# Attention and an eight-expert layer on one core: two output places used in turn, x and the routing logits in one row of 8 x 72, new step times

## The chip, the cores and the metric

One NeuronCore of a Trainium2 chip runs the whole program. The metric is device microseconds of one execution. The kernel before took 530.74 us, the median of three runs.

## The reference

The reference is an attention layer with a compressive memory, followed by a top-1 mixture of experts. There are B = 4 batches, H = 8 heads, S = 576 positions and D = 64 features of a head; then N = 2304 tokens of 512 features, E = 8 experts and F = 1024 hidden features.

```python
def _attn_ref(q, k, v, M_prev, z_prev, beta):
    scores = scale * np.matmul(q, k.transpose(0, 1, 3, 2))
    scores = np.where(causal, -1000000000.0, scores)
    scores = scores - scores.max(-1, keepdims=True)
    a = np.exp(scores)
    a /= a.sum(-1, keepdims=True) + 1e-09
    local = np.matmul(a, v)
    q_p = phi(q)
    mem_out = (q_p @ M_prev) / (q_p @ z_prev + 1e-06)
    g = 1.0 / (1.0 + np.exp(-beta))
    return g * mem_out + (1 - g) * local

def _moe_ref(x, w_gate, w1, w2):
    logits = x @ w_gate
    expert_idx = np.argmax(logits, axis=1)
    gate_w = softmax(logits)[expert_idx]
    for e in range(E):
        xe = x[expert_idx == e]
        out[expert_idx == e] = gate_w * (np.maximum(xe @ w1[e], 0.0) @ w2[e])
```

## The kernel before, in words

The program has two stages that follow each other. Attention runs from the start to about 276 us, the experts from there to the end.

**Attention** (`attention`) works on 8 groups g, each one batch and four heads, and 16 units u of two heads. For a group, q, k and v are loaded (`load`, L248 and L249, issued by SyncE), cast to 16 bits in two parts (`cast_k` L256 and L257, `cast_q` L265), and transposed by DMA (`trans`, L288, with a copy of half of it in L291) or, for the first ones, on TensorE (`ptm`, L302, L346, copied out in L305, L309, L348). `phi` (L276 to L281) makes the features for the memory. For a unit, `n_steps` makes row maxima (scores `sn` on TensorE, L375 and L381; maxima on VectorE, L383, L398, L407, L410, L411), which enter the queries as an extra column (`QT`, by DMA in L404 or on TensorE as `ptq`, L425 and L426); `s_steps` makes the scores `st` (L462), their exponentials on ScalarE (L481) and the causal cut on GpSimd (L466); `p_steps` multiplies with v (L536); `d_steps` adds up rows (`sm`, L567, evicted by ScalarE in L574). The features of v carry 8 more columns, so that a head's output has 64 numbers of x and 8 of the routing logits, 72 in all.

`m_steps(g)` has five steps, one for each tile of 128 positions (the fifth has 64). It makes the memory's part in PSUM (`ps`, 4 heads of 73), the norm (L607, L608), and two VectorE multiplies: L612 writes the 64 features of four heads into `xb` (or `xt` for the fifth tile), L614 the 8 logits of each head into `lgp`. `a_steps(g)` makes the denominators (`den`, L630 and L633, and `rl`, L635 to L639), then five times the local part (`loc`, L652), its scaling on VectorE (`lt`, L655, four heads of 72) and two additions: L659 on GpSimd to x, L662 to `lgp`, on GpSimd too but on VectorE for the last group. For each second group L668 and L670 add the logits up over the heads, and SyncE stores x to DRAM (`x_scratch`, L673 and L678). The routing (`r_...` tiles, L960 to L1076) makes ranks, tables (`r_tab`, L1051, evicted to `r_gate` in L1056 and L1057) and the token lists.

The order of all this is not that of the code. Every step has a time, computed from the table K and shifted by the entries of `sh`; the steps are sorted by it (L867), TensorE follows that list as it stands, and the other engines and the DMA queue of SyncE follow what a scheduler makes of it.

**The experts** (`experts`) are written by hand with semaphores. A turn takes 128 tokens of one expert: GpSimd gathers their rows of x (L1375), VectorE (L1586) and GpSimd (L1422) split them into two 16-bit parts, SyncE transposes them by DMA (L1298), TensorE multiplies with the first matrix (p1, L1474) and the second (p2, L1490; L1487 in a turn of 64 tokens). ScalarE evicts the result from PSUM to `ysb` (`m_y`) with the gate as its scale (L1536, or two halves in L1532), GpSimd copies the token numbers (L1399) and scatters the rows to the output (L1393). Between these, ScalarE (L1159) and VectorE (L1163) convert the next expert's weights, loaded in L1271.

There is one `ysb`. Before an eviction, ScalarE waits until the scatter before it has landed (`rr.w("sc", 16, 16)`); before a p2, TensorE waits until the eviction before it is done (`PE.wait_ge(S["ya"], yw)`). The last scatter takes its token numbers from a copy made ahead of the wait for the eviction (L1440). The first turn's x is transposed on TensorE (`m_px`, L1460).

Of the kernel before, what the change touches and what calls it, by code (L numbers as in the profile page):

```python
# [6 lines left out]
F32 = mybir.dt.float32  # L7
# [15 lines left out]
         k1=-0.85, setup=2.0, v1=2.35, sw=(3.0, 3.05, 3.1, 3.4), sm=(2.9, 3.5, 3.65), cast=-1.0, castd=0.0, tk=-0.35,
         tq=-0.45, phi=0.8, pt=1.95, lk=-1.9, lq=-1.8, lv=0.75, n=(-0.15, 0.75), s=(1.05, 2), p=(2, 3.05), m0=(4.2,
         4.1), m7=(3.35, 3.45), m=(2.6, 3.7), a0=(4.4, 4.85), a=(4, 5.2), wl=(14.4, 14.3, 15.2, 15.5, 17.0, 17.2,
         17.2, 17.6), wc=(15.8, 16.4, 16.5, 17.1, 17.3, 17.3, 18.2, 18.25), sh=dict(cast_q30=0.3, m_steps1w=0.25,
         wconv01=-0.37, load2k=-0.67, s_steps14w=-0.02, a_steps4=0.2, const_q1=-0.08, n_first68=-0.14, first_q2=0.02,
         m_steps2w=-0.15, p_steps2w=0.22, wload03=-0.05, wconv03=-0.72, s_first12=0.47, setup=-0.06, n_steps4=0.03,
         s_steps6w=-0.77, p_steps0=-0.09, s_steps13=0.03, n_steps8=-0.05, cast_k20=0.15, phi21=0.88, wload06=0.12,
         p_steps4w=0.55, a_steps1=0.15, s_steps8w=0.77, wload10=0.48, load6k=-0.18, p_steps7=0.02, s_steps4=-0.07,  # L30
         setup_w0=-0.03, n_steps15=-0.35, load4k=-0.02, n_steps13=0.17, n_steps2w=-0.2, load5q=0.25, wload02=0.03,
         p_steps12w=0.13, bothtrans_piece1=-0.03, trans3QT1=0.05, load6v=0.03, load2v=-0.28, load4q=0.08,
         wload13=-0.75, wload01=0.58, s_steps12=0.03, load1k=-0.8, m_steps7w=-0.9, s_steps1w=0.15, s_first01=0.05,
         load_pieceq0=-0.64, n_first56=0.08, p_steps1w=-0.35, m_steps5w=0.12, load0v=0.06, n_steps11=-0.43,
         load_piecek1=-0.45, wload05=-0.02, p_steps15w=0.08, n_steps12w=-0.4, s_steps3=-0.17, wconv00=-0.1,
         a_steps6w=-0.25, p_steps8w=-0.85, trans2QT1=-0.07, n_steps11w=0.05, load1q=0.6, cast_q50=0.03,
         p_steps12=0.05, p_steps9w=-0.1, phi51=0.2, wconv02=0.4, load5k=-0.12, wconv06=-0.32, phi40=-0.23,
         n_steps13w=-0.03, trans7KT1=-0.05, n_first89=0.01, phi60=-0.08, cast_q71=-0.12, setup_m2=0.05, cast_k01=0.1,
         phi50=-0.9, a_steps7=0.2, cast_q20=0.2, n_steps7=0.06, cast_q40=0.03, m_steps4=0.77, p_steps4=-0.1,
         p_steps13w=-0.4, trans7QT1=-0.02, s_first37=0.43, const_k2=-0.35, load3k=0.05, load_piecek0=-0.45,  # L40
         m_steps3=0.95, first_k2=-0.02, s_steps10w=-0.84, p_steps1=-0.06, wload04=0.1, load6q=0.05, cast_k10=0.2,
         load0k1=0.2, setup_m1=0.4, setup_w3=-0.2, p_steps13=0.4, s_steps8=0.03, setup_w2=-0.03, a_steps0w=-0.1,
         phi70=-0.7, setup_z1=0.2, wload12=0.15, a_steps3w=-0.03, s_steps9=-0.03, trans0PT=-0.01, trans4PT=-0.08,
         p_steps14=0.35, p_steps5=0.06, load4v=0.73, setup_z0=0.2, phi10=-0.08, trans2PT=-0.01, p_steps0w=-0.9,
         n_steps12=0.15, cast_k11=0.05, p_steps9=-0.1, const_k0=-0.02, load3v=-0.05, cast_q60=-0.4, wload17=0.77,
         n_steps15w=0.45, a_steps3=0.2, load3q=0.25, const_rest=-0.4, p_steps6w=-0.03, wconv05=-0.03, trans6KT1=0.13,
         phi61=-0.04, wconv04=0.17, wload07=-0.35, m_steps7=-0.43, phi01=0.15, trans4KT1=-0.07, a_steps2=-0.13,
         a_steps2w=0.43, m_steps5=0.1, s_steps12w=0.15, s_steps14=0.03, p_steps10=-0.2, n_steps4w=0.05, wload11=0.03,
         wload16=-0.03, cast_q41=0.05, cast_q21=0.03, trans5QT1=-0.2, a_steps7w=-0.1, load_piecek2=-0.77,
         s_steps7=-0.2, p_steps11w=0.07, cast_q51=-0.1, phi41=0.8, wload00=0.2, s_steps9w=0.05, p_steps8=0.7,  # L50
         bothcast_piece2=0.03, n_steps5w=-0.03, load_pieceq2=-0.8, a_steps5w=0.1, p_steps5w=0.33, s_steps1=-0.05,
         trans7PT=0.4, wconv10=0.86, m_steps4w=-0.05, cast_k50=0.05, p_steps6=0.05, s_steps13w=-0.03, load7v=-0.05,
         s_steps7w=-0.08, phi30=-0.05, s_steps4w=0.03, s_steps15=0.1, s_steps11=0.05, load5v=-0.03, m_steps6w=-0.77,
         trans3KT1=-0.05, n_first1011=0.2, p_steps10w=0.45, cast_k71=0.03, phi11=-0.2, n_steps1w=-0.03, trans6QT1=0.2,
         p_steps14w=-0.1, p_steps7w=0.83, cast_k41=-0.2, p_steps11=-0.2, d_steps3w=0.4, setup_z2=-0.4, trans3PT=-0.4,
# [1586 lines left out]
```

## Time and profile before

| | |
|---|---|
| three runs | 527.58, 530.74, 534.57 us |
| the profiled execution | 530.83 us |
| its span, first to last instruction | 529.1 us |
| mean granted TensorE clock | 0.975 |
| TensorE busy | 480.2 us, 91% of the span |
| VectorE, ScalarE, GpSimd busy | 344.1, 225.6, 260.9 us |
| instructions | 14122 |

Times in the rows are microseconds from the first instruction unless they say ns. PE is TensorE (PEld its weight load), DVE is VectorE, ACT is ScalarE, POOL is GpSimd, SPq is SyncE's issue of DMAs. A row of a timeline gives start, duration, engine, line, operation, output <- input and, in brackets, how long the engine stood idle before it and what ended that. "issue" is idle time in which the engine waited for nothing that the profile shows. The granted clock is given as a share of full speed, 2.4 GHz.

### The profile page before, as it was taken

Reading aid. Unit: us, or ns where it says so; the run is one execution under the profiler, and the core shown is the slowest. Engines: PE = TensorE matmul, PEld = TensorE weight load, DVE = VectorE, ACT = ScalarE, POOL = GpSimd, SP = SyncE. Lnnn points to the kernel's source line nnn. Section 1 sums busy time; section 2 is a strip of 40 time slices with the busy share of each in tenths; the row PEclk is TensorE's granted clock in tenths of the full one; section 3 lists DMA queues with packets and bytes.
Section 4 is the critical chain, followed back from the end, with each engine's and each line's share of the span. In section 5 each row is a group of like instructions: output and inputs, shape, how many; then the busy total and the mean of one; then the engine's idle time right before and its main releaser. Section 6 shows DMA issues by size and latency. Waiting matters only on the chain.

```text
span 529.1 us, 14122 instructions
## 1 busy us (share of the span) xinstructions
PE 480.2 (91%) x5235; PEld 323.7 (61%) x5235; DVE 344.1 (65%) x805; ACT 225.6 (43%) x360; POOL 260.9 (49%) x482
## 2 busy tenths in 40 slices
PE   4899899997989999999976999699999989999992
PEld 2454455754556565656645677477667767776872
DVE  3778686974758386889886786567752348772331
ACT  6577663753537364567523334245301033600110
POOL 5748756773729255737234343524433333453441
PEclk9989999998989999999997999999999999999997
DMA  5568969699896989996424879967896239432430
GB/s 131 126 129 170 152 146 180 145 222 159 127 190 170 169 166 176 210 290 230 164 89 86 249 249 303 238 204 230 279 269 172 93 64 299 128 109 59 100 75 26
DMA packets 169854, 89.56 MB, mean 169 GB/s; under 512 B 151855, under 2 KB 151855, under 8 KB 169776
## 3 DMA queue, kind: packets, MB, share of 16 engines
q1 hardware_dynamic: 165856, 77.62, 62.3%
q0 software_dynamic: 3920, 11.02, 6.9%
q8 instruction: 35, 0.57, 0.5%
q14 instruction: 43, 0.35, 0.2%
HBM read 54.56 MB, written 11.27 MB: 124 GB/s over the span
## 4 chain that ended last, share of the span: by engine, by line
PE 40%; issue 16%; DMA 13%; POOL 13%; DVE 7%; SPq 5%; ACT 3%; POOLq 1%; ACTq 0%; DVEq 0%
PE m_ph L1474 7%; PE o L536 6%; DMA out_dram<-m_y,m_is 5%; PE m_py L1490 5%; PE st L462 5%; PE sm L567 3%; DMA mem<-mem 3%; PE loc L652 3%; PE sn L375 2%; POOL m_xg L1375 2%; POOL m_xn L1422 2%; POOL out_dram L1393 2%; DMA QT<-mem 2%; POOL xb L659 1%; DMA m_xB<-m_xn 1%
## 5 line engine op out<-in xcount | busy, mean ns | idle before, releaser
L1474 PE MATMUL m_ph<-m_xT,mem 128*128 128x128 f16 (+1 forms) x1536 | 79.6, 214 | 7.6 <-issue 5.3
L1474 PEld LDWEIGHTS m_ph<-m_xT,mem 128*128 128x128 f16 x1536 | 77.7, 99 | 12.3 <-issue 7.1
L1579 DVE TENSOR_SCALAR m_hT<-m_ph 128x512 f16<-128x512 f32 (+1 forms) x46 | 29.1, 632 | 78.7 <-PE m_ph L1474 64.1
L1536 ACT ACTIVATE m_y<-m_py,m_gc 128x512 f32<-128x512 f32 x18 | 12.4, 688 | 132.0 <-PE m_py L1490 69.5
L1422 POOL TENSOR_TENSOR m_xn<-m_xg,m_xn 128x512 f16<-128x512 f32 x23 | 26.5, 1152 | 84.6 <-DVE m_xn L1586 84.6
L383 DVE TENSOR_REDUCE mt<-sn 128x2 f32<-128x512 f32 (+4 forms) x83 | 53.8, 666 | 21.6 <-PE sn L381 18.0
L481 ACT ACTIVATE aT<-st 128x512 f32<-128x512 f32 x96 | 55.5, 595 | 26.5 <-PE st L462 22.6
L1490 PE MATMUL m_py<-mem,m_hT 128*128 128x512 f16 x288 | 64.5, 379 | 1.3 <-issue 1.0
L466 POOL TENSOR_SCALAR_AFFINE_SELECT aT<-aT 128x128 f32<-128x128 f32 (+2 forms) x160 | 43.9, 292 | 39.8 <-ACT aT L481 38.0
L536 PE MATMUL o<-aT,mem 128*64 128x320 f32 (+4 forms) x320 | 59.3, 433 | 1.4 <-POOL aT L466 1.4
L462 PE MATMUL st<-mem 128*128 128x64 f16 (+5 forms) x224 | 46.9, 265 | 1.8 <-ACT aT L481 1.7
L1490 PEld LDWEIGHTS m_py<-mem,m_hT 128*128 128x128 f16 x288 | 27.5, 98 | 33.1 <-DVE m_hT L1579 1.3
L462 PEld LDWEIGHTS <-mem 128*128 128x128 f16 (+1 forms) x448 | 32.9, 101 | 17.0 <-issue 5.6
L462 PE MATMUL st<-QT,mem 66*128 66x64 f16 (+5 forms) x224 | 43.1, 265 | 0.1
L1474 PE MATMUL m_ph<-m_xT,m_w 128*128 128x128 f16 (+1 forms) x672 | 37.9, 220 | 4.7 <-issue 4.7
L1474 PEld LDWEIGHTS m_ph<-m_xT,m_w 128*128 128x128 f16 x672 | 37.1, 100 | 6.7 <-issue 5.5
L375 PE MATMUL sn<-mem 128*128 128x256 f16 (+3 forms) x158 | 32.5, 284 | 7.0 <-DMA mem<-mem 3.2
L1393 POOL DMA_INDIRECT out_dram<-m_y,m_is x24 | 27.7, 1153 | 21.8 <-POOL m_is L1399 12.8
L1375 POOL DMA_INDIRECT m_xg<-x_scratch,m_ig x24 | 28.5, 1187 | 19.0 <-POOL m_ig L1415 16.8
L536 PEld LDWEIGHTS o<-aT,mem 128*64 128x64 f32 x320 | 25.4, 137 | 17.4 <-issue 9.6
L659 POOL TENSOR_TENSOR xb<-lt,xb 128x256 f32<-128x256 f32 x32 | 25.3, 794 | 15.7 <-DVE lt L655 11.0
L1490 PE MATMUL m_py<-m_w,m_hT 128*128 128x512 f16 x144 | 32.2, 379 | 0.5 <-issue 0.4
(249 smaller groups left out, 943.6 us busy)
## 6 DMA issues: line engine op xcount, KB each, us to landing
mem<-in_moe_w_dram SPq DMA_DIRECT2D x40, 512.0 KB, 5.8
m_stage<-in_moe_w_dram SPq DMA_DIRECT2D x24, 512.0 KB, 6.4
mem<-in_q_dram SPq DMA_DIRECT2D x32, 128.0 KB
mem<-in_k_dram SPq DMA_DIRECT2D x32, 128.0 KB
mem<-in_v_dram SPq DMA_DIRECT2D x32, 128.0 KB
x_scratch<-xb SPq DMA_DIRECT2D x4, 1024.0 KB
mem<-mem SPq DMA_DIRECT2D x6, 288.0 KB
m_xB<-m_xn SPq DMA_TRANSPOSE x46
```

The source lines that it names most:

```text
L375: nc.tensor.matmul(ps[:, c:c + k1 - k0], QT[:, 5 * hh + t, :], keys(hh)[:, k0:k1], start=(c == 0), stop=(k1 == parts[-1][3] and hh == part ...
L383: nc.vector.reduce_max(out, v, axis=AX.X)
L462: nc.tensor.matmul(ps[:, c:c + n], kk[:, kb, :], qq[:, w:w + n], start=(first and i == 0 and j == 0), stop=(last and i == 1 and j == len(p ...
L466: nc.gpsimd.affine_select(out=ap, in_=ap, pattern=pattern, compare_op=ALU.is_ge, fill=0.0, base=base, channel_multiplier=-1)
L481: nc.scalar.activation(out=a, in_=ps, func=AF.Exp, scale=ESC)
L536: nc.tensor.matmul(o[64 * hh:64 * hh + 64, q0:q0 + n], vv, aa, start=(j == 0), stop=(j == 4), skip_group_check=True)
L659: nc.gpsimd.tensor_tensor(out=x, in0=tmp[r, :, 0:64], in1=x, op=ALU.add)
L1375: G.indirect_dma_start(out=x, out_offset=None, in_=x_dram, in_offset=bass.IndirectOffsetOnAxis(ap=i, axis=0), bounds_check=bound, oob_is_e ...
L1393: G.indirect_dma_start(out=out, out_offset=bass.IndirectOffsetOnAxis(ap=i, axis=0), in_=ysb, in_offset=None, bounds_check=bound, oob_is_er ...
L1422: G.tensor_tensor(out=xn[1], in0=xg, in1=xn[0], op=ALU.subtract).then_inc(S["xl"], 1)
L1474: mm = PE.matmul(ph[i2][:, f, 0:N], w[:, kc, c:c + 128], xT[:, x, kc, 0:N], start=(i == 0), stop=(i == 11), skip_group_check=True)
L1490: mm = PE.matmul(py, hh, ww[:, 4 + ff // 2, c:c + 512], start=st, stop=sp_)
```

## The change

First, `ysb` has two places, taken in turn, with a semaphore each (`sc0`, `sc1`). An eviction waits for the scatter two before it, in a branch that picks the place; GpSimd's `send` has the same branch and holds the copy of the token numbers, so that the copy ahead for the last scatter is gone. Second, x and its logits lie in rows of 8 heads of 72: `lgp` is gone, one VectorE multiply of 4 x 72 takes the place of L612 and L614, and one GpSimd add of 4 x 72 that of L659 and L662, for the last group too. The DRAM rows grow from 512 to 576 numbers, the gather brings all of them, and the splits read them 64 out of 72. The first turn's x goes through eight TensorE operations of a head each instead of four of 128 columns. Third, some 60 entries of the table K change.

```diff
@@ K
-         wc1=(...), nc3=2, cuts=((1, 2), (0, 1)), rc=7.75, r0=(16.1, 18.45),
-         k1=-0.85, setup=2.0, v1=2.35, ...
+         wc1=(...), nc3=2, cuts=((1, 2), (0, 1)), rc=7.75, r0=(16.0, 18.65),
+         k1=-1.2, setup=1.6, v1=2.4, ...
...
@@ m_steps
-                nc.vector.tensor_tensor(out=x[:, 64 * h0:64 * h0 + 256].rearrange("p (h d) -> p h d", d=64),
-                                        in0=ps[r, :, 0:64], in1=nrm[r].to_broadcast([n, 4, 64]), op=ALU.mult)
-                nc.vector.tensor_tensor(out=lgp[r, t, h0:h0 + 4, :], in0=ps[r, :, 64:72],
-                                        in1=nrm[r].to_broadcast([n, 4, 8]), op=ALU.mult)
+                nc.vector.tensor_tensor(out=x[:, h0:h0 + 4], in0=ps[r, :, 0:72], in1=nrm[r].to_broadcast([n, 4, 72]), op=ALU.mult)
@@ a_steps
-                x = x[:, 64 * h0:64 * h0 + 256].rearrange("p (h d) -> p h d", d=64)
-                nc.gpsimd.tensor_tensor(out=x, in0=tmp[r, :, 0:64], in1=x, op=ALU.add)
-                lp = T["lgp", b][r, t, h0:h0 + 4, :]
-                eng = nc.gpsimd if g < NG - 1 else nc.vector
-                eng.tensor_tensor(out=lp, in0=tmp[r, :, 64:72], in1=lp, op=ALU.add)
+                x = (xb[:, t] if t < 4 else xt[r])[:, h0:h0 + 4]
+                nc.gpsimd.tensor_tensor(out=x, in0=tmp[r], in1=x, op=ALU.add)
...
@@ experts
-    ysb = sb.tile([128, 512], F32, name="m_y")
+    ysb = sb.tile([128, 2, 512], F32, name="m_y")
...
-        def send(i):
+        def send():
+            def of(j):
+                i = isc[:, j:j + 1]
+                G.tensor_copy(out=i, in_=ids[:, col("c3")]).then_inc(S["iscp"], 1)
+                G.wait_ge(S["iscp"], reg["g"])
+                G.sem_inc(S["pw"], 1)
+                G.reg_add(reg[f"ns{j}"], reg[f"ns{j}"], 16)
+                G.indirect_dma_start(out=out, out_offset=bass.IndirectOffsetOnAxis(ap=i, axis=0), in_=ysb[:, j],
+                                     in_offset=None, bounds_check=bound, oob_is_err=False).then_inc(S[f"sc{j}"], 16)
             G.sem_inc(S["pw"], 1)
-            G.reg_add(reg["ns"], reg["ns"], 16)
...
+            with G.If(G.snap(reg["y"]) < 1):
+                of(0)
+                G.reg_mov(reg["y"], 1)
+            with G.Else():
+                of(1)
+                G.reg_mov(reg["y"], 0)
...
-        G.tensor_copy(out=ig0, in_=ids[:, col("c3")]).then_inc(S["iscp"], 1)
-        G.wait_ge(S["iscp"], reg["g"])
         G.wait_ge(S["ya"], reg["g"])
-        send(ig0)
-        G.wait_ge(S["sc"], reg["ns"])
+        send()
...
-        for c in range(4):
-            mm = PE.transpose(px[:, c], xg0[:, 128 * c:128 * c + 128], ident)
+        for h in range(8):
+            mm = PE.matmul(px[64 * (h % 2):64 * (h % 2) + 64, h // 2], xg0[:, h, 0:64], ident, start=True, stop=True, skip_group_check=True)
...
             rr.w("gcp", 1)
-            rr.w("sc", 16, 16)
+            def to(j):
+                A.wait_ge(S[f"sc{j}"], free)
...
+            with A.If(A.snap(odd) < 1):
+                to(0)
+                A.reg_mov(odd, 1)
+            with A.Else():
+                to(1)
+                A.reg_mov(odd, 0)
+                A.reg_add(free, free, 16)
```

What the table moves is seen in the engines' own orders. VectorE in the first 25 us, around the extra column of the first queries, before (`mt0` the maxima, `IW` a table of constants; L257 is the cast of k's second part):

```order
L407 TENSOR_TENSOR mt0_114<-mt0_114 128x5
L383 TENSOR_REDUCE mt0_114<-sn_262 128x1
L410 TENSOR_SCALAR mem81921_60<-mt0_114 128x5
L257 TENSOR_TENSOR mem81920_59<-mem81920_59 128x9x64
L411 SCALAR_TENSOR_TENSOR mem81921_60<-mt0_114,mem81921_60 128x5
L167 COPY IW_517<-ident_66 64x4x64
L309 COPY mem92162_61<-ptm_302 128x1024
```

And now, where the lines stand 3 higher:

```order
L410 TENSOR_TENSOR mt0_114<-mt0_114 128x5
L386 TENSOR_REDUCE mt0_114<-sn_262 128x1
L413 TENSOR_SCALAR mem81921_60<-mt0_114 128x5
L170 COPY IW_462<-ident_66 64x4x64
L414 SCALAR_TENSOR_TENSOR mem81921_60<-mt0_114,mem81921_60 128x5
L170 COPY IW_462<-ident_66 64x4x64
L260 TENSOR_TENSOR mem81920_59<-mem81920_59 128x9x64
L312 COPY mem92162_61<-ptm_281 128x1024
```

The cast of k's second part moved behind the instruction that completes the extra column (L411 before, L414 now); a small copy of constants stands in its place.

SyncE's queue in the middle of attention, around the store of the first batch's x, before (`mem` places are the casts, their transposes, and k, q or v as loaded):

```order
L249 DMA mem92162_61<-in_v_dram 128x1x64
L673 DMA x_scratch<-xb_930 128x4x512
L288 DMA_TRANSPOSE mem81921_60<-mem81920_59 128x18x128
L288 DMA_TRANSPOSE mem92162_61<-mem81920_59 128x18x128 x2
L248 DMA mem81920_59<-in_k_dram 128x4x64
L404 DMA_TRANSPOSE QT2_1815<-mem81921_60 128x9x128
L291 DMA mem81921_60<-mem92162_61 64x2304
L248 DMA mem81920_59<-in_k_dram 128x4x64
```

And now:

```order
L252 DMA mem92162_61<-in_v_dram 128x1x64
L407 DMA_TRANSPOSE QT2_1515<-mem81921_60 128x9x128
L291 DMA_TRANSPOSE mem81921_60<-mem81920_59 128x18x128
L667 DMA x_scratch<-xb_919 128x4x576
L291 DMA_TRANSPOSE mem92162_61<-mem81920_59 128x18x128 x2
L294 DMA mem81921_60<-mem92162_61 64x2304
L407 DMA_TRANSPOSE QT2_1825<-mem81921_60 128x9x128
L251 DMA mem81920_59<-in_k_dram 128x4x64 x2
```

One of the three transposes moved ahead of the store, and the k load that stood between the transposes and the transpose of the queries moved behind both.

TensorE at the end of attention, before (`sm` the row sums, `r_tab` the routing's table, `den` the denominators, `loc` the local part, `r_warm` matmuls whose results nobody reads):

```order
L567 MATMUL sm<-aT,ones 32x64 x4
L1051 MATMUL r_tab<-e,aT 128x288 x2
L1051 MATMUL r_tab<-q_3925,aT 128x288 x2
L1051 MATMUL r_tab<-e,aT 128x288
L630 MATMUL den<-ident,sT 128x128 x4
L633 MATMUL den_3951<-ident,sT 128x4
```

And now:

```order
L570 MATMUL sm<-aT,ones 32x64 x4
L1045 MATMUL r_tab<-q_3775,aT 128x288 x2
L629 MATMUL den<-ident,sT 128x128 x4
L632 MATMUL den_3851<-ident,sT 128x4
L1045 MATMUL r_tab<-e,aT 128x288
L651 MATMUL loc<-IW,oT 128x144 x4
L1045 MATMUL r_tab<-e,aT 128x288
L651 MATMUL loc<-IW,oT 128x144 x4
L1045 MATMUL r_tab<-q_3870,aT 128x288
```

Three of the five table rows that stood between the sums and the denominators now stand between and behind the local parts. On VectorE the two copies out of the table (L1056 and L1057, now L1050 and L1051) moved with them, from ahead of the denominators to between the logits' sums (L662, L664) and the first step of the ranks (L961, before L967).

## Rows read from the trace of the kernel before

**Rows 1.** Windows: start:end, length; busy time (instructions) of each engine; clock, DMA share, GB/s
```profile
25.00:250.00 225.00, 212.06 (x2067) 128.68 (x2066) 167.44 (x477) 131.83 (x229) 134.42 (x303) 0.98 0.85 177
290.00:529.00 239.00, 219.50 (x2784) 164.40 (x2784) 132.28 (x187) 63.23 (x76) 94.84 (x134) 0.98 0.62 175
342.00:350.00 8.00, 8.00 (x102) 7.38 (x100) 3.48 (x5) 4.58 (x5) 1.41 (x3) 0.79 1.04 228
```

**Rows 2.** Waits: engine, line, what for, total us, times, longest us
```profile
PE m_ph L1474 <- issue: 10.0, 6, 4.4
...
ACT mem L1159 <- issue: 3.6, 4, 1.4
```

**Rows 3.** Timeline of the first 25 us, SyncE, ScalarE, TensorE and VectorE
```profile
5.52 0.54 SPq L249 DMA_DIRECT2D mem<-in_q_dram  x1
...
9.27 1.16 ACT L265 ACTIVATE mem<-mem 128x1152 f16<-128x1152 f32 x1 [0.38 <-DMA mem<-in_q_dram]
...
12.26 0.26 PE L375 MATMUL sn<-mem 128*128 128x128 f16 x1 [2.33 <-ACT mem L348]
...
20.57 1.86 DVE L257 TENSOR_TENSOR mem<-mem 128x576 f16<-128x576 f32 x1
...
22.67 0.44 PE L425 MATMUL ptq<-mem 128*128 128x128 f16 x5 [1.00 <-DVE mem L411]
```

**Rows 4.** Timeline around 121 us, TensorE
```profile
121.11 0.38 PE L375 MATMUL sn<-mem 128*128 128x128 f16 x4 [1.13 <-DMA mem<-mem]
125.46 0.19 PE L501 MATMUL st<-QT,mem 66*128 66x64 f16 x1 [2.50 <-DMA QT<-mem]
```

**Rows 5.** Groups by line and shape: count, busy us, mean ns, idle before
```profile
L655 DVE TENSOR_TENSOR lt<-loc,rl 128x288 f32<-128x288 f32 x32 | 14.2, 452 | 6.6 <-PE loc L652 4.8 <-POOL lgp L662 1.3
L612 DVE TENSOR_TENSOR xb<-mem,nrm 128x256 f32<-128x256 f32 x32 | 13.4, 419 | 0.3
L614 DVE TENSOR_TENSOR lgp<-mem,nrm 128x32 f32<-128x32 f32 x32 | 5.8, 180 | 0.0
...
L659 POOL TENSOR_TENSOR xb<-lt,xb 128x256 f32<-128x256 f32 x32 | 25.3, 794 | 15.7 <-DVE lt L655 11.0 <-DVE mt L407 2.4 <-DVE nrm L608 1.6
L662 POOL TENSOR_TENSOR lgp<-lt,lgp 128x32 f32<-128x32 f32 x28 | 8.6, 309 | 0.0
```

**Rows 6.** Timeline of the end of attention, ScalarE, TensorE and VectorE
```profile
260.87 0.60 ACT L574 ACTIVATE sT<-sm 128x512 f32<-128x512 f32 x1 [1.80 <-PE sm L567]
...
263.27 0.60 PE L630 MATMUL den<-ident,sT 128*128 128x128 f32 x4
...
263.48 0.31 DVE L1056 TENSOR_SCALAR r_gate<-r_tab 128x144 f32<-128x144 f32 x1 [0.84 <-PE r_tab L1051]
...
270.08 0.20 DVE L967 TENSOR_REDUCE aT<-logits 128x5 f32<-128x40 f32 x1
```

**Rows 7.** Timeline of the experts, around 300 and 342 us
```profile
298.70 0.95 ACT L1532 ACTIVATE m_y<-m_py,m_gc 64x256 f32<-64x256 f32 x2 [11.25 <-DMA out_dram<-m_y,m_is]
299.75 2.75 PE L1490 MATMUL m_py<-mem,m_hT 128*128 128x512 f16 x12 [0.99 <-issue]
302.83 1.47 PE L1490 MATMUL m_py<-mem,m_hT 128*128 128x512 f16 x6 [0.33 <-DVE m_hT L1579]
...
341.81 7.15 PE L1474 MATMUL m_ph<-m_xT,m_w 128*128 128x128 f16 x96 [4.42 <-issue]
343.52 0.69 ACT L1536 ACTIVATE m_y<-m_py,m_gc 128x512 f32<-128x512 f32 x1 [9.57 <-DMA out_dram<-m_y,m_is]
```

**Rows 8.** Timeline of the last two scatters, GpSimd and ScalarE
```profile
515.04 0.18 POOL L1399 COPY m_is<-m_ids 128x1 int32 x1 [1.72 <-ACT m_y L1536]
516.08 1.01 POOL L1393 DMA_INDIRECT out_dram<-m_y,m_is  x1 [0.85 <-POOL m_is L1399]
519.80 0.95 ACT L1532 ACTIVATE m_y<-m_py,m_gc 64x256 f32<-64x256 f32 x2 [4.92 <-PE m_py L1487]
521.65 0.99 POOL L1393 DMA_INDIRECT out_dram<-m_y,m_ig  x1 [4.25 <-ACT m_y L1532]
```

More of the change, by code (lines that the diff above doesn't have):

```diff
@@ L23 @@
[L23 to L27, printed above, removed]
+         w2=2, wt=12, wu=5, wv=0, sz=(2.2, 2.3, 2.4, 2.2), cr=-0.55, cast1=-0.65, tk1=-0.4, phi0=0.65, pt0=1.55,
@@ L1119, in experts @@
     rp_ = sb.tile([128, rout.n2, 128], F32, name="m_rp")
-    xg0, xg = (sb.tile([128, 512], F32, name=f"m_xg{i}") for i in range(2))
+    xg0, xg = (sb.tile([128, 8, 72], F32, name=f"m_xg{i}") for i in range(2))
     xn = [sb.tile([128, 512], F16, name=f"m_xn{i}") for i in range(2)]
@@ L1131, in experts, with nat @@
     PE, A, V, G, SP = nc.tensor, nc.scalar, nc.vector, nc.gpsimd, nc.sync
+    def nat(t):
+        return t.rearrange("p (h d) -> p h d", d=64)
     idx, cnt = rout.idx, rout.cnt
@@ L1421, in turn @@
             G.wait_ge(S["txl"], reg["g16"])
-            G.tensor_tensor(out=xn[1], in0=xg, in1=xn[0], op=ALU.subtract).then_inc(S["xl"], 1)
+            G.tensor_tensor(out=nat(xn[1]), in0=xg[:, :, 0:64], in1=nat(xn[0]), op=ALU.subtract).then_inc(S["xl"], 1)
             step()
@@ L1438, in experts @@
         step()
-        G.tensor_copy(out=ig0, in_=ids[:, col("c3")]).then_inc(S["iscp"], 1)
-        G.wait_ge(S["iscp"], reg["g"])
         G.wait_ge(S["ya"], reg["g"])
-        send(ig0)
-        G.wait_ge(S["sc"], reg["ns"])
+        send()
+        for j in range(2):
+            G.wait_ge(S[f"sc{j}"], reg[f"ns{j}"])
+            G.sem_inc(S["pw"], 1)
         def warm(n):
@@ L1520, in experts @@
                 pe_body(rr, e, 1)
+        odd, free = (A.alloc_register(f"m_act_{n}") for n in ("odd", "free"))
+        A.reg_mov(odd, 0)
+        A.reg_mov(free, 16)
         def act_body(rr, half, cv, nxt):
@@ L1528, in act_body @@
             rr.w("gcp", 1)
-            rr.w("sc", 16, 16)
-            if half:
-                for o in range(2):
-                    ins = A.activation(out=ysb[0:64, 256 * o:256 * o + 256], in_=py[64 * o:64 * o + 64, 0:256], func=AF.Copy,
-                                       scale=gc[64 * o:64 * o + 64, o:o + 1])
-                ins.then_inc(S["ya"], 1)
-            else:
-                A.activation(out=ysb, in_=py, func=AF.Copy, scale=gc[:, 0:1]).then_inc(S["ya"], 1)
+            def to(j):
+                A.wait_ge(S[f"sc{j}"], free)
+                if half:
+                    for o in range(2):
+                        ins = A.activation(out=ysb[0:64, j, 256 * o:256 * o + 256], in_=py[64 * o:64 * o + 64, 0:256], func=AF.Copy,
+                                           scale=gc[64 * o:64 * o + 64, o:o + 1])
+                else:
+                    ins = A.activation(out=ysb[:, j], in_=py, func=AF.Copy, scale=gc[:, 0:1])
+                ins.then_inc(S["ya"], 1)
+            with A.If(A.snap(odd) < 1):
[3 more added lines that the diff above has]
+                to(1)
+                A.reg_mov(odd, 0)
+                A.reg_add(free, free, 16)
         for u in range(K["nc1"], done):
@@ L1541, in experts @@
         A.activation(out=xT[:, 0], in_=px, func=AF.Copy).then_inc(S["txh"], 16)
-        conv_loops(A, R(A, [(0, 1), (1, 1), (16, 16)]).start(), act_body)
+        conv_loops(A, R(A, [(0, 1), (1, 1)]).start(), act_body)
         cs = rout.counts(ctf, ccn)
@@ L1585, in dve_body @@
             rr.w("gg", 0, 16)
-            V.tensor_copy(out=xn[0], in_=xg).then_inc(S["xh"], 1)
+            V.tensor_copy(out=nat(xn[0]), in_=xg[:, :, 0:64]).then_inc(S["xh"], 1)
             h(0)
```

101 lines of the change are left out of this document (50 added, 51 removed).

## The prediction

> **What bounds the kernel now.** I read the windows by stage first. From 25 to 250 us TensorE is busy 212.06 of 225 us, VectorE 167.44, ScalarE 131.83 and GpSimd 134.42; from 290 us to the end TensorE is busy 219.50 of 239 us and no other engine as much as 60% [rows 1]. So TensorE sets the time in both stages, and any saving on another engine counts only as far as TensorE waits for that engine. There is 225 - 212.06 = 12.9 us of such waiting in the middle of attention, 19.5 us in the experts, and the start and the passage between the stages, where TensorE stands idle for short chains of small operations. Next I read TensorE's waits: the largest is "issue" ahead of p1, 10.0 us in 6 waits, the longest 4.4 us [rows 2]. Then I followed the timeline at each place that the change touches: the start [rows 3], the one long stall of the middle [rows 4], the end of attention [rows 6], the evictions of y [rows 7] and the tail [rows 8].
>
> **Two places for y.** ScalarE waits long for a scatter's landing: 11.25 us ahead of the eviction at 298.70, 9.57 ahead of that at 343.52 [rows 7]. TensorE does not pay that, since it needs the eviction only before the next p2, and a p1 lies between: p1 takes 7.15 us at 341.81 [rows 7]. It pays where the eviction comes later than that. At 298.70 + 0.95 = 299.65 the eviction ends and at 299.75 the p2 starts, after 0.99 us idle, and 0.33 us more at 302.83 for VectorE's hidden values of the same turn [rows 7]. With two places both stalls go: -1.3 us. The eviction of 343.52 moves up too, but there TensorE started its p1 at 341.81, before the eviction, so that stall of 4.42 us wasn't the eviction's; it is marked "issue" [rows 7], as are 10.0 us in 6 waits ahead of p1 [rows 2], and I leave them where they are. What is late next is the conversion of weights, which follows the eviction on ScalarE and now starts earlier.
>
> The branches are new. Behind the evictions of before ScalarE stood idle for "issue" ahead of the conversion four times, 3.6 us in all, the longest 1.4 us [rows 2]; a branch on ScalarE or GpSimd thus costs between nothing and 1.4 us. Within a turn the p1 covers it. At the end nothing does. So far the last scatter started at 521.65, 0.90 us after its eviction ended (519.80 + 0.95); the one before has 0.18 us for its copy and 0.85 us more from copy to scatter, and the copy itself began 0.16 us after its eviction (the eviction is one of 0.69 us, as at 343.52) [rows 7, 8]. That is 1.2 us instead of 0.9: +0.3. For the two branches I add 0.2 us each, near the lower end because most evictions of before show no issue time behind them: +0.7 in all, with ends at +0.3 and 0.3 + 2 x 1.4 = +3.1.
>
> [...]
>
> **x and logits in one row.** On VectorE the pair L612 and L614 costs 419 + 180 = 599 ns; the nearest row for one multiply of 4 x 72 out of PSUM is L655, 452 ns [rows 5]. That is 147 ns less, 40 times: 5.9 us of VectorE's time. On GpSimd the pair L659 and L662 costs 794 + 309 = 1103 ns; one add of 288 numbers costs between 794 ns (as if the extra 32 were free) and 1103, and in proportion to its size 893 ns, which I take: 0.21 us less, 35 times, 7.4 us. In the middle TensorE is the bound, and these are hidden but for what remains of the 12.9 us there [rows 1]; the rows name L655 as held by GpSimd's L662 for 1.3 us in all [rows 5]. I give this edit -0.5 us, with ends at 0 and -1.8 (the 1.3 and a 0.5 of shorter chains). The stores and gathers carry 576 / 512 of the bytes, 12.5% more; the gather has a turn's time and the store the rest of attention, so nothing, except for the last store, which I leave inside the range. The first turn's x goes through eight operations where four stood. Four of 128 columns in 32 bits take 0.60 us in the row of the denominators [rows 6]; eight take 1.20: +0.6, with 0 as the other end since their weight loads may overlap.
>
> **The table.** At the start, VectorE's cast L257 takes 1.86 us right ahead of L411, on which the first queries' transposes wait until 22.67 [rows 3]. The cast now stands behind: the transposes come up to 1.86 - 0.3 = 1.5 us earlier, 0.3 being the small copy that stands in its place. The copy of the transposed keys (L309) stays behind the cast, so not all of it reaches the end. Against that, the k loads now stand ahead of q's second pair on SyncE's queue. That pair's last issue was at 5.52 and its cast started at 9.27, after 0.38 us of waiting for the landing: 3.75 us after the issue [rows 3]. Three more loads of some 0.55 us each, by the row of 5.52, stand ahead of it, and the cast now stands ahead of L348, on which TensorE's first scores waited until 12.26 [rows 3]: those could come 1.9 us later. They are followed by work that waits on later loads, so I take -1.0 us for the start, with ends at -1.5 and +1.9.
>
> In the middle, TensorE waits 1.13 us for a copy of transposes and 2.50 us for the queries' transpose [rows 4], together 3.6 us. Two of the three DMA transposes now come before other loads or ahead of the k load. A stall of this kind also costs clock: after the 4.42 us at 341.81 the granted clock is 0.79 over 8 us, a part of them at 1.2 GHz instead of 2.4, which is 8 x 0.21 = 1.7 us [rows 1, 7]. The whole would be -3.6 - 1.4 = -5.0 (1.4 as 1.7 x 3.6 / 4.42). Other reorderings may open a stall elsewhere. I take half, 2.5, less the 0.5 already counted: -2.0, with ends at -5.0 and +5.0.
>
> At the end of attention the denominators started at 263.27, while the evicted sums were there at 260.87 + 0.60 = 261.47 [rows 6]; table matmuls stood between. Now one table row does: up to 1.6 us earlier, allowing 0.2 for the semaphore. The two copies of the table, 0.31 us each, now stand ahead of L967 [rows 6]: +0.6. GpSimd's five adds grow by 0.1 us each and are in a row, but start as the local parts come: +0.2 on the last. Sum -0.8, with ends at -1.6 and +0.8.
>
> **The sum.** -1.3 (stalls of y) + 0.7 (tail) - 0.5 (x row) + 0.6 (first x) - 1.0 (start) - 2.0 (middle) - 0.8 (end of attention) = -4.3 us. The profiled execution took 530.83 us, 0.1 above the median of the runs, so its span and the rest carry over: 530.8 - 4.3 = 526.5 us.
>
> **Rivals.** (a) The waits of y were hidden anyway, and the table's changes cancel: only -1.3 + 0.7 + 0.6 and the end of attention at -0.8 stay, about 530 us. For it speaks that TensorE is nearly full [rows 1]; against it the named stalls.
>
> (b) A large gain: with evictions earlier, the weights' conversions are earlier and the stall ahead of p1 at 341.81 was theirs in truth, hidden under "issue". Then 4.42 us and 1.7 us of clock go besides [rows 1, 7]: 526.5 - 6.1 = 520.4; with the whole of the middle (3.0 more) 517.4. Against it: no weight conversion ends just ahead of 341.81, as its releaser would be named.
>
> (c) Slower: the new order of SyncE's queue makes a transpose late. If one pair of stalls like those of rows 4 (3.6 + 1.4 = 5.0 us) is added in the place of the one removed and a second one elsewhere, the middle gives +5.0 in place of -2.0, and the start +1.9 in place of -1.0: 526.5 + 7.0 + 2.9 = 536.4. One such pair more than before is the point from which it decides. That the queue is the tightest resource there speaks for it; that the table moved transposes up, not down, in the place I could read speaks against.
>
> (d) The added branches make ScalarE and GpSimd stall in "issue" as TensorE does, 10.0 us in 6 waits, 1.7 us each [rows 2], and the cover fails: ten such stalls on the path are 17 us, and 543 the time. p1's 7 us of cover speak against. [...]
>
> **Chances.** Forecast 0.55, (a) 0.20, (b) 0.15, (c) 0.09, (d) 0.01. A measurement of this kernel tells about 2%, 10.6 us, from no change. Of the forecast's band hardly any is below 520.1; most of (b) is, with part of the middle's good end; (c) is partly over 541.4. So faster 0.17, within 2% 0.79, slower 0.04. The range takes the forecast, (a), most of (b) and half of (c): 516 to 534 us; the likeliest case alone spans 523 to 530.
>
> **What would show it.** Right: no eviction of y with a wait for the scatter over a few us; no stall of TensorE at the p2 near 300 us; `ptq` near 21.5 us; the denominators less than 0.5 us behind the sums' eviction; one multiply near 0.45 us and one add near 0.9 us; the end about 1.2 us from last eviction to last scatter. Wrong: the stall ahead of p1 at the second expert's start shrinking with the evictions (then b); a new wait of TensorE for a DMA of over 2 us in attention, with a clock below 0.8 behind it (then c).

## The result and the profile after

The changed kernel takes 525.64 us, the median of 20 runs (519.05 to 531.07), beside 532.89 us of the kernel before in its 20. The ratio, taken from the faster executions of each kernel, is 0.9846 with a 95% interval of 0.9811 to 0.9880 (the medians alone give 0.9864): 7 to 8 us faster, inside the stated range and within 2%. The forecast was 526.5 us, or 4.3 us faster. That the time came nearer than the gain is luck: the kernel before has 532.89 us in these 20 executions, 2.2 more than in the three that the forecast started from. The path to the time was another too, as the rows show.

The windows come first, for the two long stretches of the changed kernel. (From 25 us to the end of attention, and from the first matmul of the experts to the end. Columns as in [rows 1].)

```profile
25.00:265.88 240.88, 225.47 (x2258) 138.17 (x2254) 190.51 (x507) 143.40 (x256) 136.70 (x283) 0.99 0.86 184
267.03:521.70 254.67, 229.42 (x2913) 173.26 (x2913) 141.53 (x217) 71.28 (x83) 102.28 (x145) 0.96 0.62 171
```

The same two stretches of the kernel before:

```profile
25.00:274.87 249.87, 234.50 (x2238) 142.96 (x2236) 189.39 (x549) 142.04 (x254) 143.25 (x318) 0.98 0.81 174
276.02:529.10 253.08, 228.96 (x2901) 171.76 (x2901) 141.00 (x217) 69.54 (x83) 101.83 (x145) 0.97 0.60 169
```

The whole gain of this pair of profiles lies in attention: the experts begin at 267.03 instead of 276.02 us, 9.0 us earlier, and then take 254.67 us instead of 253.08, 1.6 longer. In attention TensorE is idle as long as before (240.88 - 225.47 = 15.4 us, 249.87 - 234.50 = 15.4); it is its busy time that fell by 9.0 us, for the same work. A part of that is clock: after its longest stall of the middle TensorE's granted clock is 0.66 from 110 to 115 us and 1.00 in the rest of this stretch; in the kernel before it was 0.67 from 30 to 35, 0.73 from 125 to 130 and 0.70 from 155 to 160 us, each with a part of its time at half of full speed. (In the first of these, at 33.36 us, the matmuls of L302, of 128 columns, start 107 ns apart, 1.2 columns a ns; at 30.54 us, at a clock of 1.00, 56 ns apart, 2.3 columns a ns.) By these shares the lower clock took some 4.5 us before and 1.7 now, an estimate. Most of the rest stands in two groups of matmuls, o and sm, before and now:

```profile
L536 PE MATMUL o<-aT,mem 128*64 128x320 f32 (+4 forms) x320 | 59.3, 433 | 1.4 <-POOL aT L466 1.4
L567 PE MATMUL sm<-aT,ones 128*32 128x64 f32 (+4 forms) x320 | 28.6, 424 | 0.1
...
L539 PE MATMUL o<-aT,mem 128*64 128x192 f32 (+4 forms) x320 | 56.3, 428 | 1.3 <-POOL aT L469 1.3
L570 PE MATMUL sm<-aT,ones 128*32 128x64 f32 (+4 forms) x320 | 25.6, 423 | 0.0
```

They are as many as before and cost 6.0 us less; e4 and e7 below ask what that is worth.

The waits of the changed kernel, TensorE's and ScalarE's:

```profile
PE m_ph L1481 <- issue: 11.7, 8, 4.5
PE sn L378 <- ACT mem L351: 6.0, 1, 6.0
PE st L504 <- DMA QT<-mem: 3.0, 3, 2.2
...
ACT m_y L1548 <- PE m_py L1497: 130.1, 17, 11.4
ACT m_y L1545 <- PE m_py L1494: 18.8, 4, 5.9
ACT m_y L1545 <- POOL m_gc L1409: 5.9, 1, 5.9
ACT mem L1156 <- issue: 5.0, 6, 1.4
```

No eviction of y waits for a scatter any more, so the two places do what they say; one waits 5.9 us for its gate (`m_gc`), a copy that GpSimd makes. The "issue" waits ahead of p1 stayed (10.0 in [rows 2], 11.7 here), and so did their longest, at the second expert's start:

```profile
326.72 0.69 ACT L1548 ACTIVATE m_y<-m_py,m_gc 128x512 f32<-128x512 f32 x1 [5.97 <-PE m_py L1497]
328.12 2.00 ACT L1156 ACTIVATE mem<-m_stage 128x1024 f16<-128x1024 f32 x2 [0.71 <-issue]
331.06 3.15 PE L1481 MATMUL m_ph<-m_xT,m_w 128*128 128x128 f16 x28 [4.52 <-issue]
```

This eviction ends 3.65 us before that p1 begins, where in [rows 7] it came after. The conversion of weights behind it starts 2.94 us before that p1; in the kernel before it started at 344.74, 2.93 us after it. The stall is 4.52 us all the same. Rival (b), that the stall was the conversions' in truth and would go with earlier evictions, falls.

The edits of x, by line:

```profile
L614 DVE TENSOR_TENSOR xb<-mem,nrm 128x288 f32<-128x288 f32 x32 | 14.4, 449 | 0.4
L657 POOL TENSOR_TENSOR xb<-lt,xb 128x288 f32<-128x288 f32 x32 | 26.5, 834 | 8.7 <-DVE lt L654 8.3 <-DVE mt L410 0.3
L1467 PE MATMUL m_px<-ident,m_xg 128*64 128x128 f32 x16 | 1.1, 279 | 0.6 <-DMA m_xg<-x_scratch,m_ig 0.6
```

One multiply takes 449 ns (452 was the row it was taken from) and one add 834 ns (893 was taken). Yet VectorE is busy 344.5 us, as before (344.1): the 40 multiplies save 6.0 us (599 - 449 ns each), and other instructions of it became longer, one of which the last section shows.

### The profile page after: what moved, and what is told of

Same layout as the page of the kernel before. It is cut to its first block, busy times and chain, and to the rows that moved or that the text cites. A ratio compares the mean times of both kernels' runs of the same rounds, so it can differ in the third digit from the quotient of the medians.

```text
span 521.7 us, 14282 instructions
## 1 busy us (share of the span) xinstructions
PE 469.3 (90%) x5247; PEld 318.7 (61%) x5247; DVE 344.5 (66%) x760; ACT 226.8 (43%) x360; POOL 254.4 (49%) x447
## 4 chain that ended last, share of the span: by engine, by line
PE 67%; DMA 8%; DVE 7%; SPq 6%; issue 5%; POOL 3%; ACT 2%; DVEq 0%; POOLq 0%; ACTq 0%
PE m_ph L1481 22%; PE m_py L1497 16%; PE o L539 6%; PE st L465 5%; SPq L251 3%; PE sm L570 3%; DMA QT<-mem 3%; PE sn L378 2%; PE m_py L1494 2%; PE loc L651 2%; DMA mem<-in_q_dram 1%; SPq L252 1%; DMA mem<-mem 1%; PE mem L605 1%; PE wm L780 1%
## 5 line engine op out<-in xcount | busy, mean ns | idle before, releaser
L1600 DVE TENSOR_SCALAR m_hT<-m_ph 128x512 f16<-128x512 f32 (+1 forms) x46 | 29.1, 633 | 83.6 <-PE m_ph L1481 75.1
L469 POOL TENSOR_SCALAR_AFFINE_SELECT aT<-aT 128x128 f32<-128x128 f32 (+2 forms) x160 | 46.6, 306 | 43.3 <-ACT aT L484 41.5
L386 DVE TENSOR_REDUCE mt<-sn 128x2 f32<-128x512 f32 (+4 forms) x83 | 53.8, 664 | 20.7 <-PE sn L384 20.0
L539 PE MATMUL o<-aT,mem 128*64 128x192 f32 (+4 forms) x320 | 56.3, 428 | 1.3 <-POOL aT L469 1.3
L378 PE MATMUL sn<-mem 128*128 128x128 f16 (+3 forms) x158 | 31.8, 280 | 8.9 <-ACT mem L351 6.0
L1372 POOL DMA_INDIRECT m_xg<-x_scratch,m_ig x24 | 26.5, 1104 | 19.3 <-POOL m_ig L1422 17.9
L539 PEld LDWEIGHTS o<-aT,mem 128*64 128x64 f32 x320 | 24.1, 137 | 18.1 <-issue 10.0
L657 POOL TENSOR_TENSOR xb<-lt,xb 128x288 f32<-128x288 f32 x32 | 26.5, 834 | 8.7 <-DVE lt L654 8.3
```

The source lines that it names most:

```text
L378: nc.tensor.matmul(ps[:, c:c + k1 - k0], QT[:, 5 * hh + t, :], keys(hh)[:, k0:k1], start=(c == 0), stop=(k1 == parts[-1][3] and hh == part ...
L386: nc.vector.reduce_max(out, v, axis=AX.X)
L469: nc.gpsimd.affine_select(out=ap, in_=ap, pattern=pattern, compare_op=ALU.is_ge, fill=0.0, base=base, channel_multiplier=-1)
L539: nc.tensor.matmul(o[64 * hh:64 * hh + 64, q0:q0 + n], vv, aa, start=(j == 0), stop=(j == 4), skip_group_check=True)
L657: nc.gpsimd.tensor_tensor(out=x, in0=tmp[r], in1=x, op=ALU.add)
L1372: G.indirect_dma_start(out=x.rearrange("p h e -> p (h e)"), out_offset=None, in_=x_dram, in_offset=bass.IndirectOffsetOnAxis(ap=i, axis=0) ...
```

## The experiments

The three parts of the change can be had apart, so six of them, with two that repeat a corner, fill the eight corners of "places for y" by "rows of 72" by "table"; the other four test a theory of TensorE's order and the start.

**e1, e2, e3: one part each.** e1 is the kernel before with the hunks of `ysb`, `isc`, `send` and `act_body`; e2 has the table K; e3 the rows of 72, with the first turn's eight operations.

```diff
-    ysb = sb.tile([128, 512], F32, name="m_y")
+    ysb = sb.tile([128, 2, 512], F32, name="m_y")
...
-         k1=-0.85, setup=2.0, v1=2.35, ...
+         k1=-1.2, setup=1.6, v1=2.4, ...
...
-            T["xb", b] = xp.tile([128, 4, 512], F32, tag="xb", name="xb")
+            T["xb", b] = xp.tile([128, 4, 8, 72], F32, tag="xb", name="xb")
```

> The kernel before with nothing but the two places for y. Theory: between the first and the last matmul of the experts the change won nothing (TensorE's stretch in the experts is 245 us before, 246 after), so the whole gain lies in attention and this kernel stays within 1.5 us of before (ratio 0.997 to 1.003), the barrier at 276 us as before, ScalarE's waits for a scatter gone (87 us before, under 5 here). Rival (the two places bring the gain): 4 us or more faster, ratio below 0.992.

Measured 527.29 us, ratio 0.9912 (0.9876 to 0.9949): the rival's value, though the interval reaches beyond 0.992. The experts take 250.83 us instead of 253.08. So the first theory, drawn from one pair of profiles, that y brought nothing, is refuted: in the changed kernel something else had hidden its gain.

> The kernel before with nothing but the new table of step times. Theory: TensorE's time in attention goes with the number of column-tiled matmul pairs (o, two heads of 64 columns) and quads (sm, four of 32) that its order tears apart: each torn one streams its columns twice, 1.05 us for 512 columns by the trace. Torn here 22 pairs and 9 quads, about 25.6 us of second streams, against 28.5 in before and 21.3 in after: 3 us faster than before, ratio 0.991 to 0.997. Rival (the table does it by other means): the whole gain, ratio 0.982 to 0.988. Rival (the saved VectorE and GpSimd work does it): no change, 0.998 to 1.002.

Measured 533.21 us, ratio 1.0016 (0.9977 to 1.0056). The new table alone brings nothing, and the theory's gain of 3 us did not come. Its step did: o and sm take 57.0 + 28.0 us, 2.9 less than before, as forecast. Attention ended 2.7 us earlier in the profile (experts from 273.35), but the time did not follow.

> The kernel before with nothing but the rows of 72 for x and logits; the old table. Theory: VectorE and GpSimd are hidden behind TensorE, and TensorE's order gets worse, 29 torn pairs and 10 torn quads, 31.6 us of second streams against 28.5: between 1 us faster and 3 us slower than before, ratio 0.998 to 1.006. Rival (the saved 6 us of VectorE and 7 us of GpSimd reach the end): 5 us faster, ratio 0.99 or less.

Measured 536.37 us, ratio 1.0085 (1.0041 to 1.0129): the rows of 72 alone cost 4.5 us, more than the theory allowed, and the rival's gain is out. o and sm take 62.8 + 28.2 us, 3.1 more than before, which is the theory's step. The experts begin at 278.16 us and take 256.14, 3.1 longer than before. Its waits:

```profile
PE m_ph L1468 <- issue: 14.5, 6, 5.5
PE sn L375 <- DMA mem<-mem: 6.0, 4, 2.4
```

Two more places show a part of the loss: "issue" ahead of p1, 14.5 us instead of 10.0, and TensorE's waits for the copies of transposes, 6.0 us instead of 3.2.

**e4, e7: sets of matmuls kept whole.** The o matmuls come in pairs (64 columns of TensorE each) and the sm matmuls in quads (32 each), and in the kernel before those for different columns stream at the same time where they stand next to each other: two of o, of 512 and 448, take 1.07 us (46.93), as one of 512 does alone (42.93). As I read its order, the scheduler tears a set when one operand is there before the others. The rows of sm show the price: alone, a matmul of 512 takes 1.05 us, four together 1.06.

```profile
86.60 1.05 PE L567 MATMUL sm<-aT,ones 128*32 128x512 f32 x2
...
88.14 1.06 PE L567 MATMUL sm<-aT,ones 128*32 128x512 f32 x8
```

(Two rows of the trace are one matmul: the first row is one of a quad, the second its other three and one of the next.) The theory was that the new order tears fewer sets. e4 writes the sets of the changed kernel in the opposite order, so that the half whose operand comes last stands first; e7 does that to the kernel before with two places.

```diff
-                for hh in range(2):
+                for hh in (1, 0):
                     vv = T["v", g][:, pr, 4 * hh + j if j < 4 else 8, :]
...
-            for c in range(4):
+            for c in (3, 2, 1, 0):
                 nc.tensor.matmul(T["sm", g][32 * c:32 * c + 32, q0:q0 + n], ...
```

> The changed kernel, with the matmuls of each pair and quad written in the opposite order, so that the scheduler tears 2 pairs and 2 quads instead of 19 and 5; the same matmuls. Theory (torn sets cost their streams): second streams fall from 21.3 to 3.9 us, of which some is given back as waits for the later operand: 8 to 17 us faster than the changed kernel, ratio to before 0.955 to 0.970. Rival (the halves were torn because an operand was late, and TensorE waits instead): as the changed kernel, 0.980 to 0.990, with TensorE idle some 10 us more in attention.

Measured 525.73 us, ratio 0.9881 (0.9838 to 0.9924): no faster than the changed kernel, as the rival said. o and sm cost TensorE less,

```profile
L539 PE MATMUL o<-aT,mem 128*64 128x320 f32 (+4 forms) x320 | 50.4, 428 | 0.3 <-POOL aT L469 0.3
L570 PE MATMUL sm<-aT,ones 128*32 128x512 f32 (+4 forms) x320 | 24.2, 423 | 1.6 <-POOL aT L469 1.6
```

50.4 and 24.2 us, where the changed kernel has 56.3 and 25.6: 7.3 us less, not half of the 17.4 that the theory had put on torn sets. And TensorE waits instead:

```profile
25.00:268.43 243.43, 219.72 (x2249) 135.10 (x2248) 186.03 (x506) 143.16 (x256) 137.42 (x283) 1.00 0.86 182
```

Busy 219.72 us, 5.8 less than the changed kernel, and idle 23.7, 8.3 more; the experts begin at 269.58.

> The kernel before with the two places for y and with its pairs and quads of matmuls kept whole (o and sm written in the opposite order), old table, old x. If streams count alone, o falls from 61.4 to 52.1 us and sm from 30.3 to 26.9: 12.7 us less TensorE work and the experts begin at 263 us. If waits take the place of two thirds of it, as in the run with the whole sets in the changed kernel (TensorE's busy time 5.8 us less, its idle time 8.3 us more), they begin at 272 us or later; ratio to before 0.985 to 0.992.

Measured 529.40 us, ratio 0.9954 (0.9910 to 0.9998), the experts from 275.49 us: the start of the second case of the expectation, with a ratio above its range. Its stretch of attention, and that of e1:

```profile
25.00:274.34 249.34, 227.62 (x2238) 139.93 (x2236) 189.62 (x549) 141.83 (x254) 142.18 (x318) 0.96 0.82 175
...
25.00:273.32 248.32, 232.72 (x2236) 141.66 (x2234) 186.46 (x548) 141.26 (x252) 141.74 (x318) 0.99 0.82 175
```

o and sm take 51.7 + 24.5 us, 11.4 less than in e1 (59.0 + 28.6). But TensorE is busy only 5.1 us less, at a granted clock of 0.96 instead of 0.99, and idle 6.1 us more. Twice, then, o and sm became 7 us or more shorter and attention no shorter.

**e6, e8: the start.** One number of the changed kernel's table loads q's second pair ahead of k; e8 adds e4's edit.

```diff
-         load0q1=0.03, n_first910=0.2, ...
+         load0q1=-0.05, n_first910=0.2, ...
```

> The changed kernel with one number of the table changed, so that the second pair of q is loaded ahead of three pairs of k instead of behind two of them. Theory: the wait of 6.0 us ahead of the first scores (15.55 us) came from that load through the cast L268 and the copy L351 behind it; the load is issued 3.3 us earlier, the first scores start at 12.3 to 13.0 us, and since TensorE is the bound from there on the experts begin 1 to 3 us earlier than 267.0; ratio to before 0.978 to 0.984. Rival (the start is caught up by 40 us anyway, as the changed kernel caught up its 3.3 us): the first scores start earlier all the same, but the experts begin where they did, ratio 0.982 to 0.988.

Measured 523.14 us, ratio 0.9843 (0.9783 to 0.9903), that of the changed kernel. The first scores came at 12.77 us instead of 15.55, the first unit's output was evicted at 36.54 instead of 38.91, and the experts began at 266.51: the 2.4 us of lead at 37 us are 0.5 at the end, and nothing in the time that can be told. The interval holds both cases; the start of the experts speaks for the rival.

> The changed kernel with both edits: whole pairs and quads, and q's second pair loaded first. Theory (TensorE the bound, edits add up): 2 us or more faster than the changed kernel, ratio 0.972 to 0.981. Rival (attention is balanced between TensorE, the DMA queue and VectorE, and the new table is fitted to the torn order): no faster than the changed kernel, 0.983 to 0.990.

Measured 526.09 us, ratio 0.9891 (0.9835 to 0.9947): the rival again.

**e5, e9 to e12: the parts in pairs.** e5 and e10 are the changed kernel with one place, e9 is the changed kernel itself beside e10 on one chip, e11 table and places, e12 rows and places; the hunks are those of e1 to e3.

> The changed kernel with y put back: one place, the copy of token numbers ahead of the last wait. The attention part is the same program as in the changed kernel. Theory (the rows of 72 and the table belong together: the table alone began the experts at 273.4, the rows alone at 278.2, both at 267.0 us): the experts begin at 267 us within 1 us, and the experts take 1 to 3 us longer than the 254.7 of the changed kernel, ratio to before 0.985 to 0.992. Rival (attention's gain was luck of that run): experts begin at 270 us or later, ratio 0.993 or more.

Measured 529.53 us, ratio 0.9976 (0.9942 to 1.0010): the rival's value, and the experts begin at 270.52 us.

> The changed kernel itself, beside the next one on one chip. Runs so far give two places for y 4.7 us alone (ratio 0.991) and, across two chips, 7 us on top of table and rows (0.998 to 0.985), while the profiles show the experts only 2.2 us shorter in either pair. Theory A (the two places bring 4 us or more): this kernel's ratio is 0.982 to 0.988 and the next one's is higher by 0.008 or more. Theory B (they bring what the experts' stretch shows, 2 us): the two ratios differ by 0.003 to 0.006.

Measured 524.53 us, ratio 0.9868 (0.9819 to 0.9917).

> The changed kernel with one place for y, beside the changed kernel on one chip. Theory A: ratio 0.994 to 1.000. Theory B: 0.986 to 0.992. The attention part is the same program as in the changed kernel, so the experts begin within 3 us of it in the profile; how far they differ shows what one profile's spread is worth.

Measured 528.47 us, ratio 0.9955 (0.9920 to 0.9989). On one chip the two differ by 0.0087, theory A, some 4.6 us; with intervals of 0.005 and 0.003 on either side theory B isn't far outside. The experts begin at 268.21 and 271.82, 3.6 us apart, more than the 3 expected.

> The kernel before with the two places and the new table, old layout of x. If the parts add up (table 1.002, places 0.991) the ratio is 0.993, and the experts begin at 272 to 275 us. If the table needs the rows of 72 to pay (as with one place: table alone 1.002, with the rows 0.998), nothing else is to be expected here either. A ratio below 0.988 would say that the rows of 72 bring nothing even with the new table.

Measured 531.36 us, ratio 0.9982 (0.9941 to 1.0023): a little more than the parts add up to, and far from 0.988. The experts began at 278.45, outside what was expected.

> The kernel before with the two places and the rows of 72, old table. If the parts add up (rows 1.008, places 0.991) the ratio is 0.997 to 1.003, and the experts begin at 276 to 279 us and take 253 to 255 us. A ratio of 0.990 or less would say that the rows cost nothing once there are two places, and that the table does not matter to them.

Measured 536.95 us, ratio 1.0066 (1.0014 to 1.0118), slower than the parts add up to; the experts from 279.95 us, for 254.45.

The corners together (ratio to before; start of the experts and their length from the profiles):

| rows | table | one place | two places |
|---|---|---|---|
| 512 | old | 1; 276.0, 253.1 | 0.9912; 274.5, 250.8 |
| 512 | new | 1.0016; 273.4, 254.7 | 0.9982; 278.5, 251.3 |
| 8 x 72 | old | 1.0085; 278.2, 256.1 | 1.0066; 280.0, 254.5 |
| 8 x 72 | new | 0.9976, 0.9955; 270.5 and 271.8, 256.8 and 255.0 | 0.9846, 0.9868; 267.0 and 268.2, 254.7 and 250.8 |

Three things follow. Two places take 1.7 to 3.4 us off the experts in each of the four pairs of a row (2.6 in the mean), and 0.002 to 0.011 off the ratio (the last row by the means of its two). The rows of 72 cost the experts 1.2 to 3.6 us in the four pairs of a column. (These are means over a spread: the changed kernel's own two profiles have 254.7 and 250.8 us.) And in attention the table and the rows pay only together: the experts begin at 275 to 279 us in the mean of the first three rows, at 269.4 in the last. The two columns of a row have the same attention steps, and still their starts differ by 1.5 to 5.1 us, now one way, now the other; the same kernel twice differs by 1.2 and 1.3 us. So one profile's start is good to some 3 us, and a pair of them, as that of the result, is no proof by itself.

The same profiles say where in attention the last row differs from the others (from 25 us to the end of attention, us; one value for each profile, in the order of the table above):

| rows | table | o and sm | TensorE idle |
|---|---|---|---|
| 512 | old | 87.9, 87.6 | 15.4, 15.6 |
| 512 | new | 85.0, 85.0 | 16.9, 21.1 |
| 8 x 72 | old | 91.0, 89.5 | 17.8, 19.8 |
| 8 x 72 | new | 81.9, 82.6, 81.9, 83.6 | 15.7, 16.5, 15.4, 15.5 |

Only with rows and table together are o and sm 4 to 6 us shorter while TensorE's idle time stays as before. In e4, e7 and e8 they are shorter still (74.6, 76.2, 75.9 us), but the idle time is 23.7, 21.7 and 20.7 us.

## Why the prediction was right, and where it was not

**Two places for y: the mechanism right, the size too small.** The term was 1.3 us for the stalls near 300 us. They are gone, and the experts shrank by 2.6 us in the mean of four pairs. Of that, TensorE's idle time is 1.5 us in the mean (0.7 to 2.4), the cost of the tail included; the rest is busy time, which differs by 3.0 us between the changed kernel's own two profiles, with the clock (229.4 us at 0.96, 226.5 at 0.98). What was left out is small: the kernel before has another stall at a p2 (0.38 us at 442.23, "issue") and one of 0.83 us at 354.97 ahead of a p1, for a weight conversion. Neither stands in e1; the changed kernel has 1.54 us of "issue" ahead of that p1.

**The tail: right.** The term was +0.7, with copy and scatter as here:

```profile
511.80 0.95 ACT L1545 ACTIVATE m_y<-m_py,m_gc 64x256 f32<-64x256 f32 x2 [4.76 <-PE m_py L1494]
513.13 0.18 POOL L1390 COPY m_is<-m_ids 128x1 int32 x1 [3.29 <-ACT m_y L1545]
514.19 0.99 POOL L1394 DMA_INDIRECT out_dram<-m_y,m_is  x1 [0.88 <-POOL m_is L1390]
```

From the eviction's end (512.75) to the scatter it is 1.44 us instead of 0.90 in [rows 8]: +0.5. That is 0.2 us above the 1.2 put down without branches, and the copy starts 0.38 us behind the eviction instead of 0.16. Rival (d) did not come.

**The rows of 72: wrong.** The step that failed was "in the middle TensorE is the bound, and these are hidden", -0.5 us, and +0.6 for the first x (+0.4 measured, 1.1 us for 0.7). Alone the rows cost 4.5 us; with the new table they bring some 0.5% of the time (1.0016 to 0.9976 and 0.9955) with one place and 1.2% (0.9982 to 0.9846 and 0.9868) with two. An edit priced by its own instructions was priced wrongly: it also made the scheduler order TensorE's work anew, as the 3.1 us more of o and sm in e3 show. Its cost in the experts was not in the sum at all; a part of it may stand in the rows as "issue" ahead of p1 (8.7 to 14.5 us in the nine profiles of kernels with rows of 72, 11.9 in the mean; 9.6 to 11.6 in the five without, 10.4 in the mean). The two sets of values overlap, and why rows of 72 should lengthen these was not tried and stays open.

**The start: wrong by sign, and without weight.** The step was that the transposes of the first queries come 1.5 us earlier, and -1.0 in the sum. They came at 24.73 instead of 22.67, 2.1 us later, by what the step had named as its other end, and put at 1.9 us at most:

```profile
13.72 1.16 ACT L268 ACTIVATE mem<-mem 128x1152 f16<-128x1152 f32 x1 [3.50 <-DMA mem<-in_q_dram]
...
15.55 0.26 PE L378 MATMUL sn<-mem 128*128 128x128 f16 x1 [6.04 <-ACT mem L351]
...
24.73 0.44 PE L428 MATMUL ptq<-mem 128*128 128x128 f16 x5
```

That cost 3.3 us at the first scores. The gain came too, and was only covered: from the first scores to the transposes it is 9.2 us instead of 10.4, and in e6, whose first scores start at 12.77, the transposes stand at 21.28. The loss was made up by 39 us, where the first unit's output is evicted 1.0 us earlier than before; e6 removed it and won nothing at the end that can be told. Neither the gain nor the loss should have gone into the sum at full size.

**The middle: right by sign, the reason not the one given.** The term was -2.0, from the stall of [rows 4]. That stall only moved (2.16 us for 2.50 at 125.46 in [rows 4]), with its clock dip behind it (the second row is a window, columns as in [rows 1]):

```profile
109.42 0.19 PE L504 MATMUL st<-QT,mem 66*128 66x64 f16 x1 [2.16 <-DMA QT<-mem]
...
110.00:115.00 5.00, 4.99 (x44) 2.92 (x43) 1.92 (x8) 3.15 (x6) 1.99 (x8) 0.66 1.10 331
```

This is the sign named for rival (c), but no second such stall came. TensorE's waits of both kinds are 5.3 us in all, 6.0 before. The whole of attention gained some 6 to 9 us, and only where table and rows come together. By the rows it went into shorter o and sm and, in part, clock, with the idle time unchanged. But e4 and e7 made o and sm shorter still and gained nothing, so fewer torn sets alone are not the cause, and the prediction's first step, that TensorE sets the time in attention, holds only in part. What keeps the waits from growing when table and rows come together, and which of the table's 60 entries do it, was not tried and stays open.

**The end of attention: right, and half the size.** The term was -0.8. The denominators follow the evicted sums (252.92) at 253.26, 0.3 us later instead of 1.8. From these sums to L961 it is 8.2 us, 8.6 before: -0.4. Of the 1.5 us won, the two table copies ahead of L961 took back 0.5, as forecast, and GpSimd's longer adds 0.5 instead of 0.2 (from the denominators' start to the last add's end 7.0 us, 6.4 before), as the logits' sums wait for them:

```profile
252.32 0.60 ACT L577 ACTIVATE sT<-sm 128x512 f32<-128x512 f32 x1 [1.76 <-PE sm L570]
253.26 0.60 PE L629 MATMUL den<-ident,sT 128*128 128x128 f32 x4
...
259.40 0.62 DVE L662 TENSOR_REDUCE logits<-xb 128x32 f32<-128x256 f32 x1 [0.29 <-POOL xb L657]
260.27 0.27 DVE L664 TENSOR_REDUCE logits<-xt 64x8 f32<-64x64 f32 x1 [0.25 <-POOL xt L657]
261.12 0.20 DVE L961 TENSOR_REDUCE aT<-logits 128x5 f32<-128x40 f32 x1
```

In all, the sum had -4.3 us in attention and nothing in the experts (-1.3 + 0.7 + 0.6). Measured are -6 to -9 in attention, and in the experts +1.6 and -2.3 by the changed kernel's two profiles. The sum came as near the measured -7 to -8 as it did by luck: an underestimated middle and an underestimated y stood against a cost of the rows in the experts that was missing and a start that did not count. Rivals (a) and (c) did not come.

No run beat the changed kernel: e6 is equal to it, e4 and e8 are equal or slower.
